# A third of the tokens between two halves of block products, weight sums in 12 places, and TensorE in source order

## The chip, the cores and the metric

The kernel runs on one core of one Trainium2 chip. The metric is device time in microseconds (us); where several runs were timed, their median. TensorE does the matrix products, VectorE (DVE), ScalarE (ACT) and GpSimd (POOL) the work on elements, SyncE (SP) issues the loads. SBUF holds the operands, PSUM the results of products.

## The reference

An attention with a learned bias, a gated layer (SiLU) behind a root-mean-square norm, and a dense mixture of four experts. The change is in the last part alone:

```python
def _moe2_ref(x, domain_probs, w1, w2):          # x: 1152 x 512, w1: 4 x 512 x 1024, w2: 4 x 1024 x 512
    p = domain_probs / (domain_probs.sum(-1, keepdims=True) + 1e-09)
    out = np.zeros((N, D), dtype=np.float32)
    for e in range(E):
        h = np.maximum(x @ w1[e], 0.0)
        out += p[:, e:e + 1] * (h @ w2[e])
    return out
```

## The kernel before

Every float32 product is made of three products in the reduced type `fp32r`: an operand is cut into an upper part (a cast on ScalarE) and a lower part (the difference, on POOL for weights, on VectorE for activations), and `three` (L773) issues hi x hi, hi x lo and lo x hi, at L775, L776 and L777.

The stage before the experts makes `y` (L931 to L952), the experts' input `x`, in four blocks of 128 columns (`e`) by three thirds of 384 tokens (`t`); a block's upper part is cast at L949, its lower part made at L950.

The stage of the experts runs over four experts, `e` (L1089). In each, `w1` is held as eight tiles of 512 x 128 (`w1_tile`), `w2` as eight tiles of 128 x 512 (`w2_tile`). `w32` (L975) brings one tile in: a load into one of four raw places, a cast (L981), a subtraction on POOL (L982); the result goes into a ring of 16 places, 13 and 3 more behind the places of the sums. Then, for each expert:

- The last third of the tokens (t = 2) is done plainly: for each of the eight `f` one PSUM tile `h2` gathers the four column blocks `c` (L1093 to L1103), 12 matmuls of 384 columns; L1099 is the ReLU and upper part, L1100 the lower part.
- `outputs(e, 2, ...)` (L1061) makes the expert's outputs for that third: three tiles of 128 tokens, 24 matmuls of 512 columns each (L1071 to L1073), then scaled by the token's probability and added up in SBUF (L1077, L1079).
- The first two thirds are done with Winograd's form of Strassen's scheme: pairs of `w1` tiles and the two thirds are cut into 2 x 2 blocks, and seven products replace eight. `token_sums` (L1024) makes the four sums of tokens once, in expert 0 (L1028, L1031, L1037, L1038), in what becomes the second `h` buffer. `sums(e, p)` (L995) makes the four weight sums of pair `p` from two raw tiles of its own: subtractions or additions on VectorE (L1009), casts (L1016), lower parts on POOL (L1017). They go into six places in turn (`n_s % 6`).
- The loop over four pairs `p` (L1111): products into `pa`, `pe`, `pb`, `pd` (six matmuls of 384 columns each). `pa` is copied out at L1118 to `c11`, gets the product with `s2` on top, is copied at L1130 to `c12`, gets `s3` on top, is copied at L1134 to `c21`. Additions from PSUM (`add_up`, L1059) make the blocks; `done` (L1052) makes the ReLU with the upper part (L1053) and the lower part (L1054). The product with `s4` on top of `pb` is kept back (`late`) and issued in the next pair, behind its first two products; for pair 3 it is issued when the loop ends. It may start only when `pb` has been read for `c22`, which takes `c21` from the copy at L1134.
- `outputs(e, 0, ...)` and `outputs(e, 1, ...)` close the expert.

In this stage the instructions' order on each engine isn't the source's: the program builder orders them itself, by the source's order as priority and by what it holds ready at a time, and it mixes the matmuls of several products. Waits between engines follow from the buffers. An engine works its queue strictly in order, and so does SP with the loads.

Of the kernel before, what the change touches and what calls it, by code (L numbers as in the profile page):

```python
# [21 lines left out]
E, F2 = 4, 1024  # L22
# [3 lines left out]
NF2 = F2 // P  # L26
TG = 384
# [34 lines left out]
class Held:  # L62

    def __init__(self, kind):
        self.kind, self.at, self.users = kind, None, 0
# [135 lines left out]
def tile_kernel(  # L201
# [20 lines left out]
    nc = tc.nc  # L222
# [625 lines left out]
    for n, (t, hp, b) in enumerate(units):  # L848
        k = POS[t] + 1
# [57 lines left out]
    def pst(name="m"):  # L907
        return psM.tile([P, 512], F32, tag="m", name=name)
# [45 lines left out]

    NW1 = 13
    ring = [bias_off[0] + 1024 * i for i in (0, 1, 2, 3, 12, 4, 5, 6, 7, 8, 9, 10, 11)]
    h_bufs = [h_off, h_off + 6144]
    acc = [at(h_off + 12288 + 512 * i, 512) for i in range(9)]  # L960
    t_off = h_off + 12288 + 4608
    s_off = t_off + 4608
    ring += [s_off + 3072 + 1024 * i for i in range(3)]
    raw_at = bias_off[0] + 1024 * 13
    raw2 = [raw_at, raw_at + 512, raw_at + 1024, gb_off]
    n_ring = n_raw2 = n_s = 0
# [21 lines left out]
    def w1_tile(e, f):  # L988
        hi, lo = w32(w1_cols(e, f), 4)
        return hi.rearrange("p (k f) -> p k f", k=4), lo.rearrange("p (k f) -> p k f", k=4)  # L990

    def w2_tile(e, f):
        return w32(w2[e, f * P : (f + 1) * P, :].rearrange("(o p) m -> p o m", o=1), 1)

    def sums(e, p):  # L995

        nonlocal n_s
        r = [raw_tile(w1_cols(e, 2 * p + i), 4) for i in range(2)]
        a11, a12, a21, a22 = (x[:, 256 * k : 256 * k + 256] for x in r for k in range(2))
        out, full = [], []  # L1000
        for i in range(4):
            off = s_off + 512 * (n_s % 6)
            n_s += 1
            s = at(off + 256, 256)
            a, b, op = (
                (a21, a22, ALU.add), (full[0] if full else None, a11, ALU.subtract), (a11, a21, ALU.subtract),
                (a12, full[1] if i > 1 else None, ALU.subtract),
            )[i]
            nc.vector.tensor_tensor(out=s, in0=a, in1=b, op=op)  # L1009
            full.append(s)  # L1010
            out.append((off, s))
        parts = []
        for off, s in out:
            t = at(off, 512, F32R)
            hi, lo = t[:, :256], t[:, 256:]
            nc.scalar.copy(out=hi, in_=s)  # L1016
            nc.gpsimd.tensor_tensor(out=lo, in0=s, in1=hi.bitcast(F32), op=ALU.subtract)  # L1017
            parts.append(tuple(x.rearrange("p (k f) -> p k f", k=2) for x in (hi, lo)))
        return parts
# [4 lines left out]
    def token_sums():  # L1024

        x = [at(h_bufs[1] + 768 * i, 768).rearrange("p (k i) -> p k i", k=2) for i in range(8)]
        for o, (hi, lo) in zip(x, (xb(0, 0), xb(0, 1), xb(1, 0), xb(1, 1))):
            nc.vector.tensor_tensor(out=o, in0=hi.bitcast(F32), in1=lo.bitcast(F32), op=ALU.add)  # L1028
        b11, b12, b21, b22, t1, t2, t3, t4 = x
        for o, a, b in ((t1, b12, b11), (t2, b22, t1), (t3, b22, b12), (t4, b21, t2)):  # L1030
            nc.vector.tensor_tensor(out=o, in0=a, in1=b, op=ALU.subtract)  # L1031
        tt = [xb(0, 1)]
        for i in range(3):
            t = at(t_off + 1536 * i, 1536, F32R).rearrange("p (a k i) -> p a k i", a=2, k=2)
            tt.append((t[:, 0], t[:, 1]))
        for (hi, lo), s in zip(tt, (t1, t2, t3, t4)):
            nc.scalar.copy(out=hi, in_=s)  # L1037
            nc.vector.tensor_tensor(out=lo, in0=s, in1=hi.bitcast(F32), op=ALU.subtract)  # L1038
        return tt

    def product(ps, a, b, onto=False):
        for k in range(2):
            three(ps, a[0][:, k], a[1][:, k], b[0][:, k], b[1][:, k], k == 0 and not onto, k == 1, onto)

    class Split:

        def __init__(self, buf, f):
            off = h_bufs[buf] + 768 * f
            t = at(off, 768, F32R)
            self.hi, self.lo, self.h = t[:, :TG], t[:, TG:], at(off + TG, TG)  # L1050

# [6 lines left out]
    def add_up(out, a, ps):  # L1058
        nc.vector.tensor_tensor(out=out, in0=ps, in1=a, op=ALU.add)  # L1059
# [26 lines left out]

    b11, b21, b22 = xb(0, 0), xb(1, 0), xb(1, 1)
    tsum = None
    for e in range(E):  # L1089
        w1t = [w1_tile(e, f) for f in range(NF2)]  # L1090
        w2t = [w2_tile(e, f) for f in range(NF2)]
        hs = []
        for f in range(NF2):  # L1093
            ps = pst("h2")[:, :TG]
            for c in range(KD):
                three(ps, w1t[f][0][:, c], w1t[f][1][:, c], xhi(c, 2), xlo(c, 2), c == 0, c == KD - 1)
            a = at(h_bufs[0] + 768 * f, 768, F32R)
            hi, lo = a[:, :TG], a[:, TG:]
            nc.scalar.activation(out=hi, in_=ps, func=AF.Relu)  # L1099
            nc.vector.scalar_tensor_tensor(  # L1100
                out=lo, in0=ps, scalar=0.0, in1=hi.bitcast(F32), op0=ALU.max, op1=ALU.subtract
            )
            hs.append((hi, lo))  # L1103
        if e == 0:
            tsum = token_sums()
        t1, t2, t3, t4 = tsum
        ready = sums(e, 0)
        outputs(e, 2, hs, w2t)
        hs = [[], []]
        late = None  # L1110
        for p in range(NF2 // 2 + 1):  # L1111
            if p < NF2 // 2:
                s1, s2, s3, s4 = ready
                half = [[tuple(w[:, 2 * k : 2 * k + 2] for w in w1t[2 * p + i]) for k in range(2)] for i in range(2)]
                c11, c12, c21, c22 = (Split(j, 2 * p + i) for i in range(2) for j in range(2))
                pa, pe_, pb, pd = (pst(n)[:, :TG] for n in ("pa", "pe", "pb", "pd"))
                product(pa, half[0][0], b11)
                nc.scalar.copy(out=c11.h, in_=pa)  # L1118
                product(pe_, half[0][1], b21)
                add_up(c11.h, c11.h, pe_)  # L1120
                c11.done()
            if late:
                s, ps, c = late
                product(ps, s, b22, True)
                add_up(c.h, c.h, ps)
                c.done()
            if p == NF2 // 2:
                break
            product(pa, s2, t2, True)
            nc.scalar.copy(out=c12.h, in_=pa)  # L1130
            product(pb, s1, t1)
            product(pd, half[1][1], t4)
            product(pa, s3, t3, True)
            nc.scalar.copy(out=c21.h, in_=pa)  # L1134
            add_up(c22.h, c21.h, pb)
            add_up(c21.h, c21.h, pd)
            c22.done()
            c21.done()
            late = s4, pb, c12
            if p + 1 < NF2 // 2:  # L1140
                ready = sums(e, p + 1)
            for j, cs in enumerate(((c11, c21), (c12, c22))):
                hs[j] += [(c.hi, c.lo) for c in cs]
        for t in range(2):
            outputs(e, t, hs[t], w2t)


def device_inputs(inputs):
# [62 lines left out]
```

## Time and profile before

| | us |
|---|---|
| median of 3 runs | 851.24 |
| lowest, highest | 851.09, 853.15 |
| the profiled execution, its own time | 853.41 |
| its span, first to last instruction | 851.6 |
| TensorE busy in the span | 812.1 |
| expert stage (first product of the last third to the end) | from 447.46 |

The table's last row is a time counted from the start of the span, as are all places in the trace. The profile is of one execution. A row in order of time gives start, duration, engine, line, operation, output and inputs, the number of instructions that it merges, and in brackets the idle time just before it with what ended it. PE's matmuls overlap, so that the start of the next one tells its pace, not its duration.

### The profile page before, as it was taken

What the parts mean: (1) busy time and instruction counts of PE and PEld (TensorE: products, weight loads), DVE (VectorE), ACT (ScalarE), POOL (GpSimd) and SP (SyncE); (2) the same over time, 40 slices, a digit from 0 to 9 for tenths busy, and PEclk for the clock granted to TensorE, in tenths of its full rate; (3) what the DMA queues carried; (4) which work ended last, traced back from release to release, by engine and by line L of the source; (5) the groups of instructions that cost most, each with busy time, mean ns of one, the idle gap of its engine ahead of it and who ended that gap; (6) DMA issues with size and microseconds to landing.
All of it is one profiled execution on the core that took longest, in us unless ns stands there. A gap on an engine that the chain in (4) does not pass through costs nothing.

```text
span 851.6 us, 15679 instructions
## 1 busy us (share of the span) xinstructions
PE 812.1 (95%) x6199; PEld 737.6 (87%) x6199; DVE 494.5 (58%) x1035; ACT 372.0 (44%) x848; POOL 311.8 (37%) x326
## 2 busy tenths in 40 slices
PE   5799999998899999999999989999899999999998
PEld 4678787877899999999999888899789888898887
DVE  7998999877857666564338274133723255332632
ACT  2488888888544434432324162222513144140510
POOL 2545363523445544542416052421605026060300
PEclk9699999999899999999999999999999999999999
DMA  6500000022323332233113032211303014041002
GB/s 235 195 3 15 3 16 3 2 77 76 99 65 109 100 95 59 94 118 109 47 34 91 21 93 62 71 53 38 112 25 112 13 50 124 0 124 38 26 1 74
DMA packets 62393, 57.09 MB, mean 67 GB/s; under 512 B 2928, under 2 KB 54640, under 8 KB 62320
## 3 DMA queue, kind: packets, MB, share of 16 engines
q1 hardware_dynamic: 62320, 56.10, 21.3%
q8 instruction: 48, 0.79, 0.4%
q14 instruction: 25, 0.20, 0.1%
HBM read 53.73 MB, written 2.36 MB: 66 GB/s over the span
## 4 chain that ended last, share of the span: by engine, by line
PE 83%; DVE 10%; DMA 2%; ACT 2%; issue 1%; SPq 1%; DVEq 0%; ACTq 0%
PE o L1071 8%; PE o L1072 8%; PE o L1073 8%; PE sc L556 4%; PE tp L626 3%; PE tp L602 3%; PE y L775 3%; PE y L776 3%; PE y L777 3%; PE tp L503 3%; PE h L776 3%; PE h L775 3%; PE h L777 3%; PE pv L776 2%; PE pg L777 2%; PE pv L777 2%
## 5 line engine op out<-in xcount | busy, mean ns | idle before, releaser
L982 POOL TENSOR_TENSOR m<-m,m 128x512 fp32r<-128x512 f32 x64 | 87.2, 1379 | 130.5 <-ACT m L981 129.8
L1071 PE MATMUL o<-m,m 128*128 128x512 f32 (+1 forms) x296 | 114.2, 388 | 0.0
L1072 PE MATMUL o<-m,m 128*128 128x512 f32 (+1 forms) x296 | 114.2, 388 | 0.0
L1073 PE MATMUL o<-m,m 128*128 128x512 f32 (+1 forms) x296 | 113.9, 387 | 0.0
L534 POOL TENSOR_TENSOR m<-m,m 128x256 f32<-128x256 f32 x84 | 69.5, 844 | 94.6 <-ACT m L531 94.5
L1017 POOL TENSOR_TENSOR m<-m,m 128x256 fp32r<-128x256 f32 x64 | 49.1, 787 | 144.0 <-ACT m L1016 134.0
L981 ACT CAST m<-m 128x512 fp32r<-128x512 f32 x64 | 39.4, 620 | 77.8 <-PE o L1073 38.3
L1079 DVE SCALAR_TENSOR_TENSOR m<-o,m,m 128x512 f32<-128x512 f32 (+1 forms) x28 | 20.2, 730 | 84.5 <-PE o L1073 84.1
L746 POOL TENSOR_TENSOR m<-m,m 128x512 fp32r<-128x512 f32 x36 | 47.1, 1311 | 57.8 <-ACT m L745 55.4
L486 DVE TENSOR_TENSOR m<-m,m 128x1024 f16<-128x1024 f16 x90 | 65.5, 742 | 1.8 <-PE tp L503 1.8
L1073 PEld LDWEIGHTS o<-m,m 128*128 128x128 f32 x296 | 55.6, 188 | 11.8
L1072 PEld LDWEIGHTS o<-m,m 128*128 128x128 f32 x296 | 55.8, 188 | 11.6
L1071 PEld LDWEIGHTS o<-m,m 128*128 128x128 f32 x296 | 55.8, 188 | 11.4
L815 POOL TENSOR_TENSOR m<-m,m 128x384 fp32r<-128x384 f32 x36 | 40.4, 1123 | 61.9 <-ACT m L814 61.9
L503 PE MATMUL tp<-m,m 128*128 128x64 f16 x1440 | 53.4, 199 | 10.0 <-DVE m L486 6.7
L503 PEld LDWEIGHTS <-m 128*128 128x128 f16 x1440 | 50.7, 102 | 12.5 <-DVE m L486 7.8
L573 ACT ACTIVATE m<-m,m 128x576 f32<-128x576 f32 x72 | 56.4, 783 | 9.4 <-DVE m L567 9.2
L1054 DVE SCALAR_TENSOR_TENSOR m<-m,m 128x384 fp32r<-128x384 f32 x64 | 48.4, 761 | 11.0 <-ACT m L1053 10.3
L567 DVE CUSTOM_DVE_ANT_0 m<-sc,m 128x576 f32<-128x576 f32 x72 | 52.3, 748 | 3.8 <-PE sc L556 3.0
L1053 ACT ACTIVATE m<-m 128x384 fp32r<-128x384 f32 x64 | 33.0, 524 | 46.7 <-DVE m L1059 45.9
L602 PE MATMUL tp<-m,m 128*128 128x128 f32 x324 | 46.8, 277 | 3.7 <-DVE m L585 1.5
L605 ACT COPY m<-tp 128x384 f32<-128x384 f32 x108 | 46.0, 487 | 8.2 <-PE tp L602 7.5
(143 smaller groups left out, 2077.5 us busy)
## 6 DMA issues: line engine op xcount, KB each, us to landing
m<-in_w SPq DMA_DIRECT2D x96, 256.0 KB, 2.8
m<-in_wg SPq DMA_DIRECT2D x12, 512.0 KB, 3.6
m<-in_wv SPq DMA_DIRECT2D x12, 512.0 KB, 3.5
m<-in_wo SPq DMA_DIRECT2D x12, 512.0 KB, 3.4
m<-in_vm SPq DMA_DIRECT2D x4, 640.0 KB, 5.2
m<-in_kt SPq DMA_DIRECT2D x4, 576.0 KB, 5.9
m<-in_qm SPq DMA_DIRECT2D x4, 512.0 KB, 7.7
out<-m SPq DMA_DIRECT2D x7, 256.0 KB, 2.0
```

Source lines behind the costliest of these rows:

```text
L486: return nc.vector.tensor_tensor(out=out, in0=d3, in1=t3, op=ALU.is_gt)
L503: nc.tensor.matmul(ps()[:, u], masks[mk.at][:, 7 - u], uvp[r], start=(r == 0), stop=(r == 1))
L534: lambda: nc.gpsimd.tensor_tensor(out=dst, in0=tmp(), in1=dst, op=ALU.add), r=[hb], w=[bk], port=True,
L567: nc.vector.tensor_tensor_reduce(out=part(hh), in0=bank_s[:, 1024 * hh : 1024 * hh + S], in1=bias[POS[t] % 2][:, 2 * hp + hh], scale=-0.12 ...
L573: nc.scalar.activation(out=part(hh), in_=part(hh), func=AF.Exp, bias=st()[:, hh : hh + 1], scale=-1.0, accum_out=st()[:, 2 + 2 * hh : 3 + ...
L602: nc.tensor.transpose(bank_t[ht.at][:, P * c : P * c + P], sps[hsp.at][:, c0 : c0 + P], ident)
L776: nc.tensor.matmul(ps, hi, ml, start=False, stop=False, skip_group_check=onto)
L777: return nc.tensor.matmul(ps, lo, mh, start=False, stop=last, skip_group_check=onto)
L982: nc.gpsimd.tensor_tensor(out=lo, in0=raw, in1=hi.bitcast(F32), op=ALU.subtract)
L1071: nc.tensor.matmul(po, hi[:, js], w2t[f][0][:, cs], start=(f == 0), stop=False)
L1072: nc.tensor.matmul(po, hi[:, js], w2t[f][1][:, cs], start=False, stop=False)
L1073: nc.tensor.matmul(po, lo[:, js], w2t[f][0][:, cs], start=False, stop=(f == NF2 - 1))
```

## The change

- The first `w1` and `w2` tiles are loaded ahead by `load_more`, in a ring of 13 places, in one list over all experts (`wanted`); `free` gives places back where the source says, and loads what fits. The room of the other three ring places goes to the weight sums, which now have 12 places.
- The order in an expert: in expert 0 the last third's products, then pairs 0 and 1, their finish, the last third's outputs, pairs 2 and 3, their finish, and the outputs of the first two thirds. In experts 1 to 3 pairs 0 and 1 come first, then the last third's products (with the finish of pair 1 behind the first of them), its outputs, pairs 2 and 3, the finish, the outputs.
- The sums for pairs 0 and 1 of the next expert are written ahead of the last outputs of an expert; those for pair p + 2 behind pair p.
- `h` blocks of pairs 0 and 1 lie in the second `h` buffer, those of pairs 2 and 3 in the first, where the last third's `h` was.
- `finish_pair` is the product with `s4`, its addition and `done`. Within a pair it stands where it did, behind the first two products.
- From the experts on, TensorE keeps the order of the source (`tc.manual_schedule` for PE alone); the other engines are ordered as before.

```diff
--- before.py
+++ after.py
@@ -954,13 +954,12 @@
-    NW1 = 13
     ring = [bias_off[0] + 1024 * i for i in (0, 1, 2, 3, 12, 4, 5, 6, 7, 8, 9, 10, 11)]
     h_bufs = [h_off, h_off + 6144]
     acc = [at(h_off + 12288 + 512 * i, 512) for i in range(9)]
     t_off = h_off + 12288 + 4608
     s_off = t_off + 4608
-    ring += [s_off + 3072 + 1024 * i for i in range(3)]
+    NS = 12
     raw_at = bias_off[0] + 1024 * 13
     raw2 = [raw_at, raw_at + 512, raw_at + 1024, gb_off]
     n_ring = n_raw2 = n_s = 0
@@ -999,7 +998,7 @@
         a11, a12, a21, a22 = (x[:, 256 * k : 256 * k + 256] for x in r for k in range(2))
         out, full = [], []
         for i in range(4):
-            off = s_off + 512 * (n_s % 6)
+            off = s_off + 512 * (n_s % NS)
             n_s += 1
             s = at(off + 256, 256)
             a, b, op = (
@@ -1044,8 +1043,7 @@
     class Split:
-        def __init__(self, buf, f):
-            off = h_bufs[buf] + 768 * f
+        def __init__(self, off):
             t = at(off, 768, F32R)
             self.hi, self.lo, self.h = t[:, :TG], t[:, TG:], at(off + TG, TG)
@@ -1086,10 +1084,24 @@
     b11, b21, b22 = xb(0, 0), xb(1, 0), xb(1, 1)
     tsum = None
-    for e in range(E):
-        w1t = [w1_tile(e, f) for f in range(NF2)]
-        w2t = [w2_tile(e, f) for f in range(NF2)]
-        hs = []
+    wanted = [(e, i, f) for e in range(E) for i in range(2) for f in range(NF2)]
+    places, w_at = [None] * len(ring), {}
+    def load_more():
+        while wanted and places[n_ring % len(ring)] is None:
+            e, i, f = k = wanted.pop(0)
+            places[n_ring % len(ring)] = k
+            w_at[k] = (w1_tile, w2_tile)[i](e, f)
+    def free(*keys):
+        for k in keys:
+            places[places.index(k)] = None
+        load_more()
+    def last_third(e, hs, frees):
+        w1t = [w_at[e, 0, f] for f in range(NF2)]
         for f in range(NF2):
             ps = pst("h2")[:, :TG]
             for c in range(KD):
@@ -1101,48 +1113,78 @@
                 out=lo, in0=ps, scalar=0.0, in1=hi.bitcast(F32), op0=ALU.max, op1=ALU.subtract
             )
             hs.append((hi, lo))
+            if f in frees:
+                free((e, 0, f))
+            if f == 0:
+                finish_pair()
+    late = []
+    def finish_pair():
+        while late:
+            s, ps, c = late.pop()
+            product(ps, s, b22, True)
+            add_up(c.h, c.h, ps)
+            c.done()
+    def pair(e, p, s, hs, tsum):
+        s1, s2, s3, s4 = s
+        t1, t2, t3, t4 = tsum
+        half = [[tuple(w[:, 2 * k : 2 * k + 2] for w in w_at[e, 0, 2 * p + i]) for k in range(2)] for i in range(2)]
+        at0 = h_bufs[1 - p // 2] + 3072 * (p % 2)
+        c11, c12, c21, c22 = (Split(at0 + 768 * i) for i in range(4))
+        pa, pe_, pb, pd = (pst(n)[:, :TG] for n in ("pa", "pe", "pb", "pd"))
+        product(pa, half[0][0], b11)
+        nc.scalar.copy(out=c11.h, in_=pa)
+        product(pe_, half[0][1], b21)
+        add_up(c11.h, c11.h, pe_)
+        c11.done()
+        finish_pair()
+        product(pa, s2, t2, True)
+        nc.scalar.copy(out=c12.h, in_=pa)
+        product(pb, s1, t1)
+        product(pd, half[1][1], t4)
+        product(pa, s3, t3, True)
+        nc.scalar.copy(out=c21.h, in_=pa)
+        add_up(c22.h, c21.h, pb)
+        add_up(c21.h, c21.h, pd)
+        c22.done()
+        c21.done()
+        late.append((s4, pb, c12))
+        for j, cs in enumerate(((c11, c21), (c12, c22))):
+            hs[j] += [(c.hi, c.lo) for c in cs]
+    pe = ctx.enter_context(tc.manual_schedule(engines={mybir.EngineType.PE}))
+    load_more()
+    ready = []
+    for e in range(E):
+        hs, hs2 = [[], []], []
         if e == 0:
+            last_third(e, hs2, ())
             tsum = token_sums()
-        t1, t2, t3, t4 = tsum
-        ready = sums(e, 0)
-        outputs(e, 2, hs, w2t)
-        hs = [[], []]
-        late = None
-        for p in range(NF2 // 2 + 1):
-            if p < NF2 // 2:
-                s1, s2, s3, s4 = ready
-                half = [[tuple(w[:, 2 * k : 2 * k + 2] for w in w1t[2 * p + i]) for k in range(2)] for i in range(2)]
-                c11, c12, c21, c22 = (Split(j, 2 * p + i) for i in range(2) for j in range(2))
-                pa, pe_, pb, pd = (pst(n)[:, :TG] for n in ("pa", "pe", "pb", "pd"))
-                product(pa, half[0][0], b11)
-                nc.scalar.copy(out=c11.h, in_=pa)
-                product(pe_, half[0][1], b21)
-                add_up(c11.h, c11.h, pe_)
-                c11.done()
-            if late:
-                s, ps, c = late
-                product(ps, s, b22, True)
-                add_up(c.h, c.h, ps)
-                c.done()
-            if p == NF2 // 2:
-                break
-            product(pa, s2, t2, True)
-            nc.scalar.copy(out=c12.h, in_=pa)
-            product(pb, s1, t1)
-            product(pd, half[1][1], t4)
-            product(pa, s3, t3, True)
-            nc.scalar.copy(out=c21.h, in_=pa)
-            add_up(c22.h, c21.h, pb)
-            add_up(c21.h, c21.h, pd)
-            c22.done()
-            c21.done()
-            late = s4, pb, c12
-            if p + 1 < NF2 // 2:
-                ready = sums(e, p + 1)
-            for j, cs in enumerate(((c11, c21), (c12, c22))):
-                hs[j] += [(c.hi, c.lo) for c in cs]
+            ready = [sums(e, p) for p in range(2)]
+        for p in range(2):
+            pair(e, p, ready.pop(0), hs, tsum)
+            if e == 0:
+                free(*((e, 0, 2 * p + i) for i in range(2)))
+            ready.append(sums(e, p + 2))
+        if e == 0:
+            finish_pair()
+        else:
+            last_third(e, hs2, range(4))
+        w2t = [w_at[e, 1, f] for f in range(NF2)]
+        outputs(e, 2, hs2, w2t)
+        for p in range(2, 4):
+            pair(e, p, ready.pop(0), hs, tsum)
+            free(*((e, 0, 2 * p + i) for i in range(2)))
+        finish_pair()
+        if e + 1 < E:
+            ready = [sums(e + 1, p) for p in range(2)]
         for t in range(2):
             outputs(e, t, hs[t], w2t)
+        free(*((e, 1, f) for f in range(NF2)))
 def device_inputs(inputs):
```

## Rows read from the trace of the kernel before

**Rows 1.** The page: busy engines, granted clock by slice, the weight loads.

```profile
PE 812.1 (95%) x6199; PEld 737.6 (87%) x6199; DVE 494.5 (58%) x1035; ACT 372.0 (44%) x848; POOL 311.8 (37%) x326
...
PEclk9699999999899999999999999999999999999999
...
m<-in_w SPq DMA_DIRECT2D x96, 256.0 KB, 2.8
```

**Rows 2.** Who TensorE waited for, 447 to 852: us in total, times, longest.

```profile
PE pa L775 <- ACT m L1130: 6.3, 4, 2.1
PE pb L775 <- ACT m L1016: 4.9, 4, 1.5
```

**Rows 3.** Stretches of experts 1 and 2: length, busy PE, PEld, DVE, ACT, POOL, clock.

```profile
547.70:649.40 101.70, 98.52 (x482) 88.36 (x481) 39.76 (x65) 31.61 (x69) 32.99 (x33) 0.98 0.22 63
649.40:749.60 100.20, 97.00 (x482) 86.86 (x481) 40.94 (x65) 31.39 (x68) 33.14 (x33) 1.00 0.21 63
```

**Rows 4.** TensorE in order of time, expert 1: start, duration, instruction, wait.

```profile
604.90 0.34 PE L777 MATMUL pb<-m,m 128*128 128x384 f32 x1
606.99 0.44 PE L775 MATMUL pa<-m,m 128*128 128x384 f32 x1 [1.75 <-ACT m L1130]
607.27 0.34 PE L776 MATMUL pa<-m,m 128*128 128x384 f32 x1
...
609.02 0.52 PE L775 MATMUL pd<-m,m 128*128 128x384 f32 x1
609.34 0.52 PE L776 MATMUL pd<-m,m 128*128 128x384 f32 x1
```

**Rows 5.** VectorE and TensorE in order of time before the first wait of expert 2.

```profile
698.45 1.46 DVE L1009 TENSOR_TENSOR m<-m,m 128x256 f32<-128x256 f32 x1
...
700.40 0.45 PE L775 MATMUL pb<-m,m 128*128 128x384 f32 x1 [1.49 <-ACT m L1016]
```

**Rows 6.** In order of time around the first expert product: four engines.

```profile
439.74 0.96 DVE L1031 TENSOR_TENSOR m<-m,m 128x768 f32<-128x768 f32 x1 [3.45 <-PE y L777]
...
447.65 3.91 DVE L1031 TENSOR_TENSOR m<-m,m 128x768 f32<-128x768 f32 x2
...
451.49 0.54 DVE L950 TENSOR_TENSOR m<-y,m 128x384 fp32r<-128x384 f32 x1
...
447.66 0.48 ACT L949 CAST m<-y 128x384 fp32r<-128x384 f32 x1 [0.56 <-PE y L777]
...
447.18 7.51 POOL L982 TENSOR_TENSOR m<-m,m 128x512 fp32r<-128x512 f32 x4 [2.22 <-ACT m L981]
...
447.46 0.34 PE L775 MATMUL h<-m,m 128*128 128x384 f32 x1
...
449.22 0.34 PE L776 MATMUL h<-m,m 128*128 128x384 f32 x1
```

**Rows 7.** In order of time: the first pair of expert 0 and its copy.

```profile
481.92 0.34 PE L777 MATMUL pa<-m,m 128*128 128x384 f32 x1
...
482.35 0.48 ACT L1118 COPY m<-pa 128x384 f32<-128x384 f32 x1 [17.30 <-PE pa L777]
```

**Rows 8.** Groups by line, 447 to 852: busy us, mean ns, idle before.

```profile
L1059 DVE TENSOR_TENSOR m<-pb,m 128x384 f32<-128x384 f32 x32 | 17.7, 554 | 52.3 <-ACT m L1134 29.4 <-PE pb L777 22.4
...
L1134 ACT COPY m<-pa 128x384 f32<-128x384 f32 x16 | 7.6, 473 | 27.5 <-PE pa L777 27.5
```

**Rows 9.** In order of time, end of expert 0's outputs and after: ACT, POOL, DVE.

```profile
548.97 0.62 ACT L981 CAST m<-m 128x512 fp32r<-128x512 f32 x1 [0.68 <-DMA m<-in_w]
...
550.40 0.62 ACT L981 CAST m<-m 128x512 fp32r<-128x512 f32 x1 [0.81 <-DMA m<-in_w]
...
543.71 10.04 POOL L982 TENSOR_TENSOR m<-m,m 128x512 fp32r<-128x512 f32 x8 [24.69 <-ACT m L981]
...
554.82 0.42 DVE L1009 TENSOR_TENSOR m<-m 128x256 f32<-128x256 f32 x1 [1.57 <-DMA m<-in_w]
```

**Rows 10.** Who ScalarE waited for, 447 to 852: the loads of weights.

```profile
ACT m L981 <- DMA m<-in_w: 26.0, 26, 3.7
```

## The prediction

> **What bounds the kernel now.** I read the page first: TensorE (PE) is busy for 95% of the span and its granted clock is 9 tenths or more in every slice but one [rows 1]. So the kernel is bound by TensorE, and a change that keeps every product can only win back TensorE's idle time. The second view was who waits for whom, with TensorE alone and the expert stage alone: eight waits, two in each expert, 6.3 us on a copy of `pa` (L1130) and 4.9 us on a cast of a weight sum (L1016) [rows 2]. Third, the expert stage in one stretch per expert: 101.7 us for expert 1, 100.2 us for expert 2, with TensorE busy for 98.5 and 97.0 [rows 3]. Fourth, the waits in order of time [rows 4]. The gap behind 604.90 shows that a wait costs more than its figure: the next product starts at 606.99, 2.09 us after the last one, where 0.18 is normal (447.46 to 449.22 are ten [rows 6]), and it takes 0.28 itself, so 2.01 us are lost where the row says 1.75. The wait is counted from the modelled end of a matmul, 0.16 after its slot, and the restart costs 0.10. Eight waits of 11.2 us thus lose 11.2 + 8 x 0.26 = **13.3 us**. This wait is followed by a stretch in which a product takes 0.32 instead of 0.18: TensorE ran at the lower of its two levels (1.2 of 2.4 GHz). That stretch is why expert 1 is 101.7 - 100.2 = **1.5 us** longer than expert 2, and the clock of its row is 0.98 [rows 3, 4]. Together 14.8 us are to be had, 1.7% of the time.
>
> What makes the waits: [rows 5] shows the first one of expert 2. The sum of weights (L1009) for the last pair is made at 698.45, as late as its place lets it, takes 1.46 us, goes through a cast, and TensorE stands for 1.49 us. There are six places for sums and a pair needs four, so pair p+1 is not prepared before pair p has used its own.
>
> **The change, part by part.** Products, loads (96 of 256 KB), casts and subtractions stay the same in number and size; only order and places change.
>
> Sums in 12 places, pairs in two halves: sums for two pairs are ready before the first pair, and each later pair has the last third's products and outputs or the earlier pairs in front of it. The waits on L1016 go. The waits on L1130 go too, since they come at the end of a chain that starts with the same late sums and with copies that run behind them. I take all 13.3 us and the 1.5 us of the low clock away: **-14.8**.
>
> Source order on TensorE, start of expert 0. The last third's first product begins at 447.46, right behind the `y` products. After nine matmuls it comes to the fourth column block; the second matmul of that one, at 449.22, needs the lower part of the last `y` block (L950). VectorE makes that at 451.49, behind two token differences (L1031) that take 3.91 us together, against 0.96 for one at 439.74, because POOL subtracts at the same time [rows 6]. Before, TensorE went on with the first three column blocks of other products and lost nothing. In source order it stands until 452.08, 2.9 us. The ring has 13 places instead of 16, so POOL has two subtractions there and not four, and the second difference ends a little sooner: I take **+2.6**. The bounds are 0 (VectorE does L950 first: the cast of 447.66 ends at 448.14, and 0.54 more is 448.7, in time) and 2.9. I take the upper part because nothing in the change alters what VectorE has ready at 447.65.
>
> The finish of a pair (`finish_pair`: the product with s4 on top of `pb`). TensorE may not write `pb` until VectorE has read it, and VectorE waits for the copy c21 out of `pa`. From the last matmul's slot to the copy's start is 0.25 us (481.92 + 0.18 to 482.35) [rows 7], the copy takes 0.47, the addition 0.55 [rows 8], two handovers of some 0.04 and the restart 0.10: 1.46 us (an estimate from these rows). Inside a pair of halves two products of 1.05 each cover it: 2.1 against 1.36. Behind pair 3 nothing covers it, as the source has the finish before the outputs: once in each expert, and once more in expert 0, where the outputs follow pair 1: 5 x 1.46 = **+7.3**. It cannot be less; one more VectorE operation of 0.55 in front would make it 10.1. In experts 1 to 3 the finish of pair 1 stands behind the last third's first product (2.1 us) and is covered.
>
> Beginnings of halves, eight of them. The copy c11 needs 0.25 + 0.48 + 0.05 = 0.78, the product between takes 1.05 [rows 7]: covered if ScalarE is free. In experts 1 to 3 the first pair follows the outputs, and there ScalarE is casting the next weights as they land: at 548.97 and 550.40, with waits of 0.68 and 0.81 for the load [rows 9]. A copy ready 1.3 us after the end of the outputs (547.7 [rows 3], so 549.0) comes behind the cast of 548.97: done at 550.1 instead of 549.7, 0.4 us late with the restart; if also behind the cast of 550.40, 1.8; if ahead of both, 0. I take 0.4 three times: **+1.2**, between 0 and 5.4.
>
> The border of pairs 0 and 1 in experts 1 to 3. Here VectorE works on the sums for pair 2, whose load comes 7.1 us after the outputs' end (554.82, after a wait of 1.57) [rows 9]. The addition that frees `pb` is ready at about 7.5 and has 0.75 us to spare. Four sums of 0.42 in front of it, at the doubled length that [rows 6] shows beside POOL 0.8, make it up to 1.2 us late; none if it goes first. I take the middle, 3 x 0.6 = **+1.8**, between 0 and 3.6.
>
> Three w2 tiles of an expert are loaded later (ring of 13): their places come free in pairs 0 and 1 of expert 0, or in the last third's first three products, and they are read 3.5 to 4.9 us into the outputs; a cast (0.62) and a subtraction (10.04 / 8 = 1.25) fit there [rows 9]. Taken at 0; with the cover gone one such step, 1.9 us and the load. The loads stay in one order on SP, the order of the raw places; behind a load that waits there stand only later weights, as in the kernel before. The moved `h` buffers are written after their last reader in every case: 0.
>
> Sum against the profiled execution: 853.41 - 14.8 + 2.6 + 7.3 + 1.2 + 1.8 = 851.5, that is -1.9. The profiled execution is 2.17 us above the median of 851.24. If the median has the low stretch of expert 1 as well, the result is 849.3; if it doesn't, 850.8. I put **849.8**.
>
> A rule weighed: the difference L1031 takes 0.96 with POOL idle and 1.95 beside its subtractions [rows 6]. The Trainium skill, "SBUF — State Buffer", section "Who interferes with whom", says that a VectorE instruction with two SBUF inputs and a POOL instruction that reads SBUF use one port pair, and that the one which comes second is blocked for the whole of the other. By that rule each of the four sums could stand for a whole subtraction, 4 x (0.42 + 1.25) = 6.7 us where the doubled length of the rows gives 3.4; the border would then cost 3 x 4.5 instead of 3 x 0.6, and the time would come out as in the third case below.
>
> **The rivals.** Second case, a clear gain: VectorE does L950 ahead of the differences, and the start costs nothing: 849.3 - 2.6 = **846.7** (848.2 without the low stretch). For it: L950 comes earlier in the source, and its input (448.14) is there before the second difference starts, 1.95 us behind the first [rows 6]. Against it: with the same inputs the order before was the other one.
>
> Third case, slower: queues of ScalarE and VectorE in the first two pairs of experts 1 to 3, which now stand where eight subtractions (10.04 us) and late loads are, and where before only the last third's products stood, which need nothing at once. Price: the copy behind both casts, 1.8, and the border at the top of its range, 1.2, then the same again at pair 1's finish, some 2: 5 us in each of three experts, 15 instead of 3.0, so +12 on 849.8, of which a part overlaps: I put **857**. For it: ScalarE waited 26 times for a weight load, up to 3.7 us [rows 10]. It turns to slower once these waits exceed 2.3 us per expert (849.8 + 3 x 1.3 = 853.8).
>
> Fourth case, nothing moved: the wait of 2.6 us and the five finishes call up the low clock again (+1.5, as behind the 1.75 us wait [rows 4]) and give back the rest: **851.2**.
>
> **How the numbers follow.** A measurement of this kernel can tell about 0.3% (2.6 us) from no change, so faster means below 848.7 and slower above 853.8. Forecast (849.8, own range 847.5 to 852.5): 0.42, a quarter of it below 848.7. Second case: 0.27, nine tenths of it below. Third: 0.17. Fourth: 0.14. Faster 0.42 x 0.25 + 0.27 x 0.9 = 0.35; slower 0.17; within 0.3%: 0.48. The range from 846.2 to 854.0 leaves out some 0.08 below (the second case with a cheaper border) and 0.12 above (most of the third).
>
> **What would show it.** Right: no wait of TensorE on L1016; a wait of about 1.2 us on VectorE's addition from `pb` (1.46 with what the row leaves out) in front of the finish behind pair 3, four times, and one behind pair 1 in expert 0; one of 2 to 3 us some 1.7 us into the first `h` product. Wrong: no wait there (second case); waits on the c11 copy or on `pb` at the borders of pairs 0 and 1 of more than 2 us per expert (third); a slice of lower clock just behind 449 (fourth). A wait of TensorE for a w2 tile in the outputs would be a cost that I have at zero.

## The result and the profile after

| | before | after |
|---|---|---|
| median, us | 851.16 (4 runs) | 861.9 (4 runs) |
| lowest, highest | 849.06, 853.15 | 861.06, 864.13 |
| ratio, 95% interval | | 1.0131, 1.0098 to 1.0163 |
| the profiled execution | 853.41 | 861.06 |
| expert stage, first product to start of last matmul | 447.46 to 848.17: 400.7 | 445.53 to 855.85: 410.3 |

The change makes the kernel slower by 10.7 us, 1.3%. The forecast was 849.8 with a range to 854.0; "slower" had a chance of 0.17. The stage of the experts is 9.6 us longer between the two profiled executions, so nearly all of the loss lies there.

The page of the kernel after, engines and granted clock by slice (answers to [rows 1]):

```profile
PE 814.7 (95%) x6199; PEld 738.1 (86%) x6199; DVE 488.5 (57%) x1035; ACT 373.0 (43%) x848; POOL 314.1 (37%) x326
...
PEclk9699999999999999999999999999999999999999
```

The same 6199 matmuls, and the clock looks untouched in the slices. So the loss must be idle time again. Who TensorE waited for, 440 to 870, in us in total, times and longest (answers to [rows 2]):

```profile
PE pb L775 <- DVE m L1057: 14.0, 8, 2.9
PE h L776 <- DVE m L950: 2.7, 1, 2.7
PE pa L775 <- ACT m L1140: 0.7, 2, 0.4
```

Neither row of [rows 2] is left. No wait is on a weight sum or on its copy now, so the removed 11.2 us are really gone. In their place stand 17.4 us on other things, and the largest is the one that I had priced at five waits: the product of `finish_pair` on top of `pb` waits for VectorE's addition from `pb` (L1057, which was L1059). There are eight such waits, and the longest is 2.9 us where I had 1.2.

I measured each wait as the prediction does, from the start of one matmul to the start of the next, less the normal 0.18 (and give the 0.10 of the restart apart):

| where | us lost by starts | forecast, restart included |
|---|---|---|
| second matmul of the fourth column block, expert 0 | 2.83 | 2.6 |
| finish of pair 1, expert 0 | 1.32 | 1.46 |
| finish behind pair 3, experts 0, 1, 2 | 3.02 each | 1.46 each |
| finish behind pair 3, expert 3 | 1.32 | 1.46 |
| finish of pair 1 behind the last third's first product, experts 1 to 3 | 1.19, 1.21, 1.21 | 0 |
| copy c11 in the first pair, experts 1 to 3 | 0.54, 0.46, 0.28 | 0.4 each |
| borders of pairs 0 and 1, experts 1 to 3 | 0 | 0.6 each |

These are 19.4 us by starts, and about 0.10 for each of twelve restarts, 1.2. Two stretches at the lower clock come on top. Engine time in chosen stretches (length, PE, PEld, DVE, ACT, POOL, clock, DMA):

```profile
450.70:454.10 3.40, 3.40 (x13) 3.40 (x12) 3.40 (x7) 1.62 (x3) 0.95 (x1) 0.50 0.17 49
617.90:621.30 3.40, 3.10 (x9) 2.90 (x10) 2.68 (x6) 1.23 (x3) 1.03 (x2) 0.51 0.49 138
```

Clock 0.50 is TensorE's lower level (1.2 of 2.4 GHz). A product of 384 columns starts every 0.32 us there instead of every 0.18, and by starts each stretch loses 1.5 us, as the one before did; twice, 3.0. The slices of the page, 21 us long, don't show it. In all 19.4 + 1.2 + 3.0 = 23.6 us are lost in the stage, against 14.8 before: 8.8 more, and the stage grew by 9.6.

**A wait of 2.86 us, and the one of 1.16 us beside it.** TensorE in order of time, kernel after, end of pair 3 in expert 0:

```profile
513.37 0.34 PE L777 MATMUL pa<-m,m 128*128 128x384 f32 x1
516.56 0.44 PE L775 MATMUL pb<-m,m 128*128 128x384 f32 x1 [2.86 <-DVE m L1057]
```

ScalarE over the same time:

```profile
512.25 0.39 ACT L1015 CAST m<-m 128x256 fp32r<-128x256 f32 x1
512.96 0.41 ACT L1015 CAST m<-m 128x256 fp32r<-128x256 f32 x1 [0.32 <-DVE m L1008]
513.27 0.62 ACT L980 CAST m<-m 128x512 fp32r<-128x512 f32 x1
514.83 0.71 ACT L1015 CAST m<-m 128x256 fp32r<-128x256 f32 x2 [0.95 <-DVE m L1008]
515.45 0.47 ACT L1150 COPY m<-pa 128x384 f32<-128x384 f32 x1
```

VectorE over the same time:

```profile
512.51 0.41 DVE L1008 TENSOR_TENSOR m<-m,m 128x256 f32<-128x256 f32 x1
512.85 1.09 DVE L1052 SCALAR_TENSOR_TENSOR m<-m,m 128x384 fp32r<-128x384 f32 x1
513.86 0.94 DVE L1008 TENSOR_TENSOR m<-m,m 128x256 f32<-128x256 f32 x1
515.95 0.56 DVE L1057 TENSOR_TENSOR m<-pb,m 128x384 f32<-128x384 f32 x1 [1.15 <-ACT m L1150]
```

POOL, beside VectorE's last two rows before its wait:

```profile
512.72 1.80 POOL L1016 TENSOR_TENSOR m<-m,m 128x256 fp32r<-128x256 f32 x2 [1.68 <-ACT m L1015]
```

By the prediction's 0.25 the copy c21 (L1150) could start at 513.37 + 0.18 + 0.25 = 513.80. It starts at 515.45, 1.65 us later. From 513.89 to 514.83 ScalarE stands idle with that copy behind it, because the next instruction in its queue is a cast of a weight sum (L1015) whose last sum (L1008) VectorE makes only at 513.86, slowed to 0.94 us beside POOL. These are the sums for the first pair of the *next* expert. In the source they stand behind the finish. The builder has moved them up, and free places let it. The first pair of expert 1, which reads them, begins some 35 us later. VectorE itself stands idle for 1.15 us until the copy is there.

Expert 3 has no next expert. The same place there, TensorE:

```profile
819.62 0.34 PE L777 MATMUL pa<-m,m 128*128 128x384 f32 x1
821.12 0.45 PE L775 MATMUL pb<-m,m 128*128 128x384 f32 x1 [1.16 <-DVE m L1057]
```

Here nothing stands ahead of the copy (it starts at 820.00, 0.20 behind the slot), and the wait is the 1.2 us that the prediction names.

### The profile page after: what moved, and what is told of

It reads as the page before. It is cut to its first block, busy times and chain, and to the rows that moved or that the text cites. A ratio compares the mean times of both kernels' runs of the same rounds, so it can differ in the third digit from the quotient of the medians.

```text
span 859.3 us, 15710 instructions
## 1 busy us (share of the span) xinstructions
PE 814.7 (95%) x6199; PEld 738.1 (86%) x6199; DVE 488.5 (57%) x1035; ACT 373.0 (43%) x848; POOL 314.1 (37%) x326
## 4 chain that ended last, share of the span: by engine, by line
PE 53%; issue 22%; DVE 12%; POOL 6%; DMA 5%; ACT 2%; SPq 0%; DVEq 0%; POOLq 0%; ACTq 0%
POOL m L981 4%; PE sc L556 4%; DMA m<-in_w 3%; PE tp L602 3%; PE tp L626 3%; PE tp L503 3%; PE y L777 3%; PE y L775 3%; PE y L776 3%; PE pv L777 2%; PE pg L776 2%; PE pv L775 2%; PE pv L776 2%; PE pg L775 2%; PE pg L777 2%
## 5 line engine op out<-in xcount | busy, mean ns | idle before, releaser
L1016 POOL TENSOR_TENSOR m<-m,m 128x256 fp32r<-128x256 f32 x64 | 51.5, 830 | 37.5 <-ACT m L1015 37.5
L1052 DVE SCALAR_TENSOR_TENSOR m<-m,m 128x384 fp32r<-128x384 f32 x64 | 43.0, 676 | 11.6 <-ACT m L1051 11.3
L556 PE MATMUL sc<-m,m 64*128 64x64 f32 (+3 forms) x320 | 48.3, 451 | 0.5 <-DMA m<-in_kt 0.5
```

Of the source, the lines that this page charges most:

```text
L556: nc.tensor.matmul(o, w, ks_t[hp][rows, b, j : j + n], start=True, stop=True)
```

## The experiments

Theory **A**: casts of early sums stand ahead of a copy that TensorE waits for; ScalarE's strict order turns early, unhurried work into a wait. Theory **B**: VectorE's own work and its slowing beside POOL makes the addition late, wherever ScalarE's casts stand. A further question stands over both: what does the one line that fixes TensorE's order cost by itself? The texts on record below were written before each run; where they name further theories, they say which. Each ratio is to the kernel before, timed beside the run on the same chip (851.6 to 851.9 us). The kernel after was not timed again there, so that differences from its 861.9 compare two occasions.

**The next expert's sums behind the copy.** In ScalarE's queue alone, the casts of the next expert's sums are put behind the last copy c21. In the trace VectorE keeps its order, and POOL's subtractions of these sums follow their casts.

```diff
-        nc.scalar.copy(out=c21.h, in_=pa)
+        last_copy.append(nc.scalar.copy(out=c21.h, in_=pa))
...
         if e + 1 < E:
-            ready = [sums(e + 1, p) for p in range(2)]
+            with tc.issue_after(last_copy[-1].ins):
+                ready = [sums(e + 1, p) for p in range(2)]
```

> The changed kernel, with the next expert's weight sums (their casts on ScalarE) queued behind the copy of c21 of pair 3. TensorE's and VectorE's work is the same. Theory A (ScalarE's queue: in experts 0 to 2 casts of sums stand in front of the copy that the finish of pair 3 waits for): the three waits of 2.9 us fall to about the 1.2 us of expert 3, 5.1 us less, some 857. Theory B (VectorE and POOL slow each other there, so the sums and the additions are late whatever the queue of ScalarE holds): the three waits stay above 2.3 us, 860 to 862. Theory C (the source order alone costs, wherever a finish stands): no change, 862.

Measured: 854.1 us, 1.0035 of before (1.0017 to 1.0053), 7.8 us under the kernel after and 2.9 under what A said. ScalarE in order of time at the same place:

```profile
512.02 0.48 ACT L1150 COPY m<-pa 128x384 f32<-128x384 f32 x1 [0.44 <-PE pa L777]
512.40 1.32 ACT L1015 CAST m<-m 128x256 fp32r<-128x256 f32 x4
```

TensorE there:

```profile
511.65 0.34 PE L777 MATMUL pa<-m,m 128*128 128x384 f32 x1
513.14 0.44 PE L775 MATMUL pb<-m,m 128*128 128x384 f32 x1 [1.16 <-DVE m L1057]
```

The four casts now run behind the copy in one go, and the three gaps of 3.02 are 1.32 each: 5.1 us. The low clock behind 617 went too, 1.5, which A's price had left out; that makes 6.6, and the stage is 403.75 instead of 410.3, 6.6 less. VectorE still makes all four sums ahead of the addition, from 508.63 to 512.00. With POOL's subtractions moved back as well, the last sum takes 0.41 here instead of 0.94. But in the kernel after VectorE was idle for 1.15 us in front of the addition, waiting for the copy: the slower sum counted only because the copy stood behind its cast. A holds, and B falls for these three waits.

**An expert's own sums as well.** The same for the casts of the sums for pairs 2 and 3, which are written behind pairs 0 and 1.

```diff
-            ready.append(sums(e, p + 2))
+            with tc.issue_after(last_copy[-1].ins):
+                ready.append(sums(e, p + 2))
```

> As the run before, and the sums for pairs 2 and 3 of an expert queued behind the c21 copy of pairs 0 and 1 too. Theory A: the waits of the finish of pair 1 behind the last third's first product (1.2 us in experts 1 to 3) go as well, another 3.6 us, some 853. Theory B: they stay, 857 to 860, since the sums still run beside POOL. Theory C: no change.

Measured: 849.12, 0.9962 (0.9944 to 0.9979), 5.0 us under the run before where A said 3.6; the stage is 3.3 shorter (400.5). The three waits at the finish of pair 1 behind the last third's first product are gone; L1057 has 5.8 us in five waits left, the five that the prediction counted. In the kernel after, ScalarE showed the same picture there:

```profile
567.11 0.71 ACT L1015 CAST m<-m 128x256 fp32r<-128x256 f32 x2 [1.41 <-DVE m L1008]
567.73 0.47 ACT L1150 COPY m<-pa 128x384 f32<-128x384 f32 x1
```

With ScalarE's queue mended at these two places the kernel stands at 849.1, near the 849.8 that I had forecast without them, with the start, five short finishes and the copies c11 still in it.

**The finish inside the outputs.** The product with `s4` is issued behind the first tile of the outputs, so that its chain runs beside 24 output matmuls; ScalarE's queue is left alone.

```diff
     def outputs(e, t, hs, w2t, then=None):
         for j in range(3):
+            if j == 1 and then:
+                then()
...
-        if e == 0:
-            finish_pair()
-        else:
+        if e:
             last_third(e, hs2, range(4))
...
-        finish_pair()
...
-            outputs(e, t, hs[t], w2t)
+            outputs(e, t, hs[t], w2t, finish_pair)
```

> The changed kernel with the finish of pair 3 (and of pair 1 in expert 0) behind the first of three output tiles instead of ahead of it: 5.6 us of output products stand between the copy and the finish. Theory A and B: the five waits (1.2, 2.9, 2.9, 2.9, 1.2 us as the trace counts them, 12.2 us with restarts) go, 861.9 - 12.2 = 849.7. Theory C, and a rival by which the outputs themselves then wait for the late blocks of pair 3: less than half of it comes back, 856 or more.

Measured: 846.68, 0.9935 (0.9912 to 0.9959), 15.2 us under the kernel after. Who TensorE waited for:

```profile
PE pb L775 <- DVE m L1057: 3.0, 3, 1.1
PE h L776 <- DVE m L950: 2.7, 1, 2.7
```

All five finishes that stood uncovered are free, whatever stands ahead of the copy: 3 x 3.02 + 2 x 1.32 = 11.7 by starts, 0.5 of restarts, 1.5 of clock, 13.7 together, and the stage is shorter by 13.4 (396.9). The forecast of 849.7 had left out the clock; the rest of the 15.2 doesn't show in the stage of the profiled executions. This one move is worth more than the whole difference between before and after.

**The last column block later.** In expert 0 the first three blocks of three products go first, then their fourth blocks.

```diff
+            if e == 0:
+                if f == 0:
+                    for g in range(3):
+                        columns(g, range(KD - 1))
+                columns(f, range(KD - 1 if f < 3 else 0, KD))
```

> The changed kernel with the first three column blocks of three products ahead of the fourth block of the first in expert 0's last third, which gives VectorE 4.7 us more for the last lower part. Theory: the wait of 2.7 us at the start goes (2.9 with its restart), and with it the stretch at the lower clock behind it (1.7 us where it came): 857.3 to 859.0. Rival: the wait only moves to the next product, because VectorE is behind with its token sums altogether: 861 or more.

Measured: 859.8, 1.0094 (1.0072 to 1.0116), only 2.1 us under the kernel after and between the two forecasts. The wait at the start, 2.67, is gone and the low clock behind it too, 2.9 + 1.5. But the stage is only 1.3 us shorter (409.0): 2.4 go to a new wait in the first pair, some 0.7 to small ones in experts 1 and 2. TensorE, then ScalarE:

```profile
463.33 0.34 PE L777 MATMUL pe<-m,m 128*128 128x384 f32 x1
465.77 0.44 PE L775 MATMUL pa<-m,m 128*128 128x384 f32 x1 [2.10 <-ACT m L1153]
```

```profile
463.87 0.41 ACT L1015 CAST m<-m 128x256 fp32r<-128x256 f32 x1 [0.80 <-DVE m L1008]
464.18 0.48 ACT L1124 ACTIVATE m<-h 128x384 fp32r<-128x384 f32 x1
464.57 0.40 ACT L1015 CAST m<-m 128x256 fp32r<-128x256 f32 x1
464.86 0.49 ACT L1124 ACTIVATE m<-h 128x384 fp32r<-128x384 f32 x1
465.24 0.48 ACT L1153 COPY m<-pa 128x384 f32<-128x384 f32 x1
```

TensorE comes to the first pair earlier by what it saved, and meets ScalarE still at sum casts, which wait for VectorE (whose sums had waited 1.48 us for a load). The copy c11 could have started soon after the last matmul into `pa` (462.28) and starts at 465.24. Twelve casts of sums stand ahead of it, and the first two pairs need eight: four belong to a later pair. So it is theory A's mechanism a third time, at another copy (two ReLU of the last third, L1124, stand there too): a wait taken away at one place comes back at the next place where the same queue is late.

**The builder's order on TensorE.** The change without its last line, nothing else.

```diff
-    pe = ctx.enter_context(tc.manual_schedule(engines={mybir.EngineType.PE}))
```

> The changed kernel without the one line that holds TensorE to the source's order: 12 places for sums, the pairs in two halves and the ring of 13 stay. Theory A (what costs is a finish, or the start, exposed in a fixed order behind a copy that stands late in ScalarE's queue): the builder fills these gaps with other products, the five waits at a finish, the three at the last third and the one at the start shrink to under 5 us together, 843 to 849. Theory C (the order of the blocks itself, or sums still late for their places, costs): waits of more than 10 us remain, 852 or more.

Measured: 835.37, 0.9804 (0.9762 to 0.9845): 26.5 us under the kernel after, and 16.5 under the kernel before on the same chip (851.9). It is the fastest kernel here and beats both. A named the direction, but its range began 7.6 us higher. The trace names no wait of TensorE in the whole stage. The stage in one stretch, this kernel (columns as above):

```profile
444.80:832.00 387.20, 387.15 (x1946) 348.65 (x1944) 164.08 (x269) 122.57 (x264) 121.99 (x117) 1.00 0.21 61
```

and the kernel after:

```profile
445.50:856.10 410.60, 393.10 (x1946) 351.07 (x1944) 161.78 (x268) 122.39 (x264) 122.65 (x117) 0.99 0.20 58
```

The same 1946 matmuls; ScalarE, VectorE and POOL are as busy as there. ScalarE's queue isn't mended either. ScalarE, this kernel:

```profile
503.46 0.41 ACT L1015 CAST m<-m 128x256 fp32r<-128x256 f32 x1 [1.47 <-DVE m L1008]
503.77 0.62 ACT L980 CAST m<-m 128x512 fp32r<-128x512 f32 x1
504.30 0.40 ACT L1015 CAST m<-m 128x256 fp32r<-128x256 f32 x1
505.15 0.71 ACT L1015 CAST m<-m 128x256 fp32r<-128x256 f32 x2 [0.45 <-DVE m L1008]
505.77 0.47 ACT L1150 COPY m<-pa 128x384 f32<-128x384 f32 x1
```

Four casts ahead of the copy again, but TensorE has other work meanwhile:

```profile
504.51 0.34 PE L777 MATMUL pa<-m,m 128*128 128x384 f32 x1
...
505.56 0.33 PE L777 MATMUL pa<-m,m 128*128 128x384 f32 x1
505.74 0.40 PE L1070 MATMUL o<-m,m 128*128 128x512 f32 x1
...
510.17 0.39 PE L1071 MATMUL o<-m,m 128*128 128x512 f32 x1
510.40 0.34 PE L775 MATMUL pb<-m,m 128*128 128x384 f32 x1
```

The copy L1150 starts too early for the product that ends with 505.56, which is another pair's; it reads the one that ends with the matmul of 504.51. It could start at 504.51 + 0.18 + 0.25 = 504.94 and starts at 505.77, 0.83 us late. Until the next matmul into `pb`, the finish, TensorE does that other product and 20 output matmuls, the latter 4.7 us long. So a late copy is a cost only where the source order leaves TensorE nothing else to do: A is right on where the copy is late, and the fixed order is what turns the lateness into idle time.

**Source order kept, all places mended.** The finish in the outputs, the last block later, the finish of pair 1 behind the last third's second product instead of its first, and the own sums behind the copy. The first two are as in the diffs above; the others:

```diff
-            if f == 0:
+            if f == 1:
                 finish_pair()
...
-            ready.append(sums(e, p + 2))
+            with tc.issue_after(last_copy[-1].ins):
+                ready.append(sums(e, p + 2))
```

> The changed kernel with four edits: the finish of pair 3 (and of pair 1 in expert 0) behind the first output tile, the finish of pair 1 in experts 1 to 3 behind the second product of the last third instead of the first, the fourth column block later at the start, and the sums for pairs 2 and 3 queued behind the c21 copy of pairs 0 and 1. Theory A: of TensorE's waits only the c11 copies at the first pair of experts 1 to 3 are left, 1.3 to 2 us together, and no stretch of lower clock in the experts; the kernel with the finish in the outputs is at 846.7, the start gives 2.9 to 4.6 and the last third's finish 3.5 to 3.9: 838 to 841. Rival: the waits move to the next product that needs ScalarE or VectorE: 844 or more.

Measured: 838.92, 0.9848 (0.9815 to 0.9881). All that TensorE waits for in the stage is

```profile
PE pa L775 <- ACT m L1155: 1.0, 3, 0.4
```

the copy c11 in experts 1 to 3. Four edits by hand win back 23 of the 26.5 us that the line costs.

**Nine places instead of twelve**, in source order:

```diff
-    NS = 12
+    NS = 9
```

> The changed kernel with nine places for sums instead of twelve. Theory A: the places only matter where they let a sum run ahead of its need. The next expert's first sums still find four places free in pair 3, so the three long waits of the finish (2.9 us) stay, and so do those at the last third: 859 to 863. Rival D (twelve places, by letting sums run early, are what makes the long waits): they shrink to 1.2 us, 857 or less.

Measured: 858.59, 1.0089 (1.0059 to 1.0118). The result stands between the theories. The three waits behind pair 3 are as long as with twelve places, so nine are enough to let the next expert's sums run early. The three waits in front of the last third's second product are gone (L1057: 11.3 us in five waits); there ScalarE does the copy between the casts:

```profile
565.58 0.41 ACT L1015 CAST m<-m 128x256 fp32r<-128x256 f32 x1 [0.40 <-DVE m L1008]
565.89 0.47 ACT L1150 COPY m<-pa 128x384 f32<-128x384 f32 x1
566.46 0.71 ACT L1015 CAST m<-m 128x256 fp32r<-128x256 f32 x2
```

**The kernel before with the one line.** The order of the source on TensorE, six places, pairs not in halves.

```diff
+    ctx.enter_context(tc.manual_schedule(engines={mybir.EngineType.PE}))
     for e in range(E):
         w1t = [w1_tile(e, f) for f in range(NF2)]
```

> The kernel before with that one line alone: TensorE in source order from the experts on, sums in six places, four pairs in a row. Theory A: the start costs its 2.9 us here as well, and each expert's last finish is exposed behind pair 3 (about 1.4 us, four times), and each pair but the first waits for sums that its own places hold up: TensorE waits for 25 us or more, 860 or more. Theory C: the same loss as in the changed kernel, about 862. A rival by which the blocks' order in two halves is what costs: the time of the kernel before, 849 to 853.

Measured: 857.7, 1.0068 (1.0044 to 1.0093), less than A and C said and more than the rival. Who TensorE waited for:

```profile
PE pb L775 <- DVE m L1059: 10.7, 7, 1.9
PE h L776 <- DVE m L950: 2.7, 1, 2.7
PE pa L775 <- ACT m L1131: 2.3, 5, 1.0
PE pa L775 <- ACT m L1119: 0.5, 2, 0.3
```

The wait at the start comes with the line alone, 2.7 us, as forecast for it. The rows of [rows 2] don't stay as they were with the line's waits added: the sum's cast (L1016 there) ends no wait any more, and the copy of [rows 2] 2.3 us instead of 6.3. That is where the sum of both, on which the expectations went, was too high. The line costs 5.8 us in the old structure (857.7 - 851.9, the median of before on that chip) and 26.5 in the new one.

**Nine places, the builder's order.**

```diff
-    NS = 12
+    NS = 9
...
-    pe = ctx.enter_context(tc.manual_schedule(engines={mybir.EngineType.PE}))
```

> The changed kernel in the builder's order, with nine places for sums instead of twelve. If the two halves are what keeps the sums in time (eight places are needed for two pairs, the rest only lets sums run early): no wait of TensorE, 834 to 837. If it takes the twelve places: waits on casts of sums come back, 839 or more.

Measured: 837.1, 0.9831 (0.9789 to 0.9874), and no wait of TensorE in the stage. The interval overlaps that of twelve places, so the last three places bring nothing that these runs can tell. How much of the gain is the halves and how much the places beyond six isn't separated. The kernel before with twelve places was written for that, but its six extra places overlapped memory that was still in use; there is no time for it, and the question stays open.

## Why the prediction was wrong, point by point

**What is removed: right.** I took away 14.8 us for the sums in time and the pairs in halves. The kernel with just that (the builder's order) is 16.5 us under before, its stage 13.8 shorter (386.9 for 400.7), with no wait left.

**What source order costs: the term that was mis-sized.** I had 2.6 + 7.3 + 1.2 + 1.8 = 12.9 us, and the line costs 26.5 between the medians, 23.4 between the stages of the two profiled executions (410.3 and 386.9). Of the other 3.1, 2.3 come from the executions profiled, which lie 0.8 below and 1.5 above their medians; 0.8 stay open. In the stage:

- *The start*, 2.6: it lost 2.83 + 0.10. Right in place and size; the second case (nothing there) fell. The row of TensorE after shows the matmul where the prediction put it:

```profile
450.12 0.45 PE L776 MATMUL h<-m,m 128*128 128x384 f32 x1 [2.67 <-DVE m L950]
```

- *Five finishes at 1.46*, 7.3: right for two (1.32 + 0.10 each). The same part of the other three, 1.42 each, is there as well, 7.1 together. The step that failed is the bound behind it, "one more VectorE operation of 0.55 in front would make it 10.1". I looked for what could stand ahead of the addition on VectorE, and not for what could stand ahead of the copy on ScalarE: three finishes lost 1.70 more each, **5.1**. Putting the casts behind the copy took this away.
- *The finish of pair 1 in experts 1 to 3*, "covered": it lost 1.2 each with the cover of 2.1 us in place, **3.9** with restarts. It is covered as forecast once the sums stand behind the copy, so the cover was counted rightly and the queue ahead of the copy wasn't.
- *The copy c11*, 1.2: 1.28 by starts, 1.6 with restarts. Right, and by the mechanism named, a weight cast that waited for its load (ScalarE, kernel after):

```profile
552.78 0.62 ACT L980 CAST m<-m 128x512 fp32r<-128x512 f32 x1 [0.97 <-DMA m<-in_w]
553.31 0.47 ACT L1140 COPY m<-pa 128x384 f32<-128x384 f32 x1
```

- *The border of pairs 0 and 1*, 1.8: nothing was lost. The lower bound was the value.
- *The low clock*, counted only in the fourth case with 1.5: two stretches, **3.0**. One follows the wait at the start, which was that case's sign, one a finish of 3.02 in expert 1.
- *Three w2 tiles later*, at nothing: no wait. Right.

What I had priced and what came of it: 2.9 + 7.1 + 1.6 + 0 = 11.6, against 12.9. What I hadn't: 5.1 + 3.9 + 3.0 = 12.0. Together 23.6, what the stage loses by the trace.

**The third case** said slower, 857, through ScalarE's and VectorE's queues in the first two pairs of experts 1 to 3. The engines and the sort of cause were right, the places in part. In each of these experts the copy c11 lost 0.4 to 0.6 where the case had 1.8, the border nothing where it had 1.2, and the finish of pair 1 lost 1.3 where it had some 2. The largest new cost came where the case didn't look, behind pair 3. The case's price before the overlap was taken off, 861.8, is close to the measured 861.9 by luck. I had read the 12 places only as a cure (sums in time) and not as room in which the builder, which orders ScalarE still, may move casts ahead of anything whose input isn't there yet.

**The rule weighed.** A sum (L1008) takes 0.41 at 512.51 and 0.94 at 513.86, beside POOL's subtractions (512.72 to 514.52); the doubled length of [rows 6] was a fair price. The rule of the Trainium skill, "SBUF — State Buffer", section "Who interferes with whom", would have let each wait for a whole subtraction; 0.53 more is less than the 0.90 of one such subtraction; it would fit the rest of one that had begun, but these rows don't show that it is. The border's price by that rule, 3 x 4.5, didn't come: nothing was lost there. With that price the prediction's sum gives 861.5, not the 857 of the third case; that this is near the measured time is luck too.

The Trainium skill, "PSUM — Partial Sum Buffer", section "Engine vs sequencer instructions", says that ScalarE's queue is strictly first in, first out. The trace agrees: the copy L1150 starts 1.65 us after it could, behind the casts, and for 0.95 of these ScalarE is idle.

**What stood in no case of mine:** that the rest of the change wins 2% by itself and the last line loses more than that. [rows 6] showed the means for it: before, TensorE lost nothing at the `y` block, because it took other products. I priced each place where the source leaves a gap, and not the loss of the ability to fill a gap that I hadn't seen.

## What to carry to other kernels

When one engine's order is fixed by hand, list for each point where it waits everything that another engine's queue may hold ahead of the releasing instruction, and first of all the unhurried work that new buffers allow to run early; either hold that work behind the instruction, or put enough other products at that point. More places for a result are not only a cure: an engine that works in order pays when work from the future comes in front of work that is waited for. Test a fixed order and a new structure apart: here the structure won 16.5 us and the order lost 26.5 (in the older structure 5.8).

## What the runs showed of the hardware

Behind some waits TensorE fell to its lower level for a stretch of about 3.4 us, and behind others not: in the kernel after, gaps of 2.83 (expert 0's start) and 3.02 (expert 1) were followed by one, gaps of 3.02 in experts 0 and 2 weren't, and before, the gap of 1.91 in expert 1 was [rows 4] while those of 2.29 and 1.87 in experts 0 and 2 weren't. With nine places in source order the same wait at the start (2.7 us) was followed by a granted clock of 1.00. Each such stretch cost 1.5 us, and the length of the wait alone doesn't tell whether it comes.
